# Routing intermediates and bias in PSUM, the blank of the scatter table in parts, rank matmuls one slot later

## The chip, the core and the metric

One core of one Trainium2 chip runs the whole program. Its engines work side by side: PE (TensorE, matmuls and transposes), DVE (VectorE), ACT (ScalarE), POOL (GpSimd) and SP (SyncE, which here only issues DMAs). The metric is the device time of one execution in microseconds; lower is better.

## What is computed

The reference is attention in chunks, then two mixtures of experts (MoE), each of which sends a token to the one expert with the highest logit:

```python
# attention: 8 batches, 8 heads, 576 positions, head size 64, chunks of 64
scores = scale * matmul(q_c, k_c.T)            # 64 x 64 per chunk and head
attn = exp(scores - max); attn /= attn.sum(-1) + 1e-9
x = matmul(attn, v_c)                          # -> x: 4608 tokens x 512
# MoE: 8 experts, 512 -> 1024 -> 512
logits = x @ w_gate + modality_bias[modality_id]
e_idx = argmax(logits)
gate_w = max of softmax(logits)
out[mask] = gate_w * (relu(x[mask] @ w1[e]) @ w2[e])   # for each expert e
# MoE2: the same without bias, for tokens with x @ w_skip > 0, and out = x + y
```

## The kernel before

The change touches the attention stage, about the first 200 us. It walks over 36 tiles of 128 tokens (`for t in range(NTILE)`, L724). One turn of the loop issues, on PE and in this order: the scores of tile t+2 (`sc`, L494, one PSUM bank, one buffer), the transposes of half of the next k (`ps_t<-rk`, L465), the transposes of the probabilities of tile t+1 (`ps_p`, L520), those of the finished rows x of tile t-1 (`ps_x`, L554), those of half of the next q (`ps_t<-rq`), and the product with v (`o_ps`, L529, two PSUM banks, of which each row uses 260 of 512 columns). DVE takes the row maximum `mx` and the difference `e` of the scores, and divides the product by the row sums (`rs`, `x`). ACT takes the exponential and copies out of PSUM. POOL reorders each k and q load (`rk`, `rq`, L457: a sum of two SBUF operands). SP issues all loads.

Every four tiles give a group of 512 tokens, which is routed by the generator `route(gi)` (L566), nine in all. In tiles with t % 4 == 1, from 5 on, PE makes the partial logits (`ps_l`, L560). Then the generator runs in slots: each call of `drip()` in the loop (after `sc`, after `mx`, after `e`, between the three operations of the division, and after them) runs it to its next `yield`, so its instructions lie between those of the tile. In order they are: transposes of the logits (`ps_l2`, named `ps_l` with a number, L571); on DVE their sum `lgt` and the bias added (L578); `gate_argmax`, which is `r_mx`, `r_d` = logits less maximum, `r_er`, on ACT `r_ex` = exp(`r_d`), then `r_mr`, the one-hot choice `r_oh`, the sum `r_sm` of `r_ex`, and its reciprocal into `row`; then `wait2` empty slots; then on PE the rank matmuls `ps_r` (`ranks_mm`, L245, 14 small ones from `r_oh`); on DVE `ranks` (`r_z`, `pos`, `carry`) and `posi`; and on POOL four scatters of `row` into the table `tab` in DRAM (L600).

The pool `ps_l` has one PSUM bank, used in turn by `ps_l`, `ps_l2` and `ps_r`. The intermediates `lgt`, `r_d`, `r_er`, `r_ex`, `r_sm`, `r_z`, `pos` lie in SBUF (pool `rt_p`). Route 3 also picks the fullest expert (`GP` = 3), whose first weight is then loaded, cast by ACT and split (`w1s`, L637) half by DVE and half by POOL in the turns that follow.

Work that is done once, in `g.late`, is run three entries per turn. Among it stands `tables()` (L164), which fills the two tables with a blank by two DMAs on SP, and `bias()` (L175), which computes the bias of all tokens with one transpose and five DVE operations.

Of the kernel before, what the change touches and what calls it, by code (L numbers as in the profile page):

```python
# [131 lines left out]
def setup_late(nc, g, tmp, modality_id, modality_bias, w_gate2, w_skip):  # L132

    NT, NTILE, DM = g.NT, g.NTILE, g.DM
    md = tmp.tile([NTILE, P, 2], I32, name="md")
    nc.gpsimd.dma_start(
        out=md, in_=modality_id.bitcast(I32).rearrange("(t p w) -> t p w", p=P, w=2)
    )
    b01 = tmp.tile([P, 2, E], F32, name="b01")
    nc.gpsimd.dma_start(  # L140
        out=b01.rearrange("p m e -> p (m e)"),
        in_=modality_bias.rearrange("m e -> (m e)").unsqueeze(0).to_broadcast([P, 2 * E]),
    )
# [12 lines left out]
    n = g.NR // P
    m = next(i for i in range(10, 0, -1) if n % i == 0)
    blank0 = tmp.tile([P, n // m, 16], I32, name="blank0")
    nc.gpsimd.memset(blank0, 0)
    nc.gpsimd.memset(blank0[:, :, 0], int(OOB))  # L160
    for t in g.row4:
        nc.gpsimd.memset(t, 0)

    def tables():  # L164
        nc.sync.dma_start(
            out=g.tab[0].rearrange("(p m n) c -> p m (n c)", p=P, m=m),
            in_=blank0.rearrange("p n c -> p (n c)").unsqueeze(1).to_broadcast([P, m, n // m * 16]),
        )
        nc.sync.dma_start(out=g.tab[1].rearrange("(p n) c -> p n c", p=P), in_=blank)

    nop = lambda: None

    mf = tmp.tile([NTILE, P], F32, name="mf")

    def bias():  # L175
        pm = g.ps_l.tile([P, P], F32, tag="l", name="pm")
        nc.tensor.transpose(pm[:, 0:NTILE], mf, g.ident[0:NTILE, 0:NTILE])
        m = tmp.tile([P, NTILE, 2], F32, name="m")
        nc.vector.tensor_copy(m[:, :, 1], pm[:, 0:NTILE])
        nc.vector.tensor_scalar(  # L180
            out=m[:, :, 0], in0=m[:, :, 1], scalar1=-1.0, scalar2=1.0, op0=ALU.mult, op1=ALU.add
        )
        t0 = tmp.tile([P, NTILE, E], F32, name="t0")
        sh = [P, NTILE, E]
        for i, dst in ((0, t0), (1, g.bias)):
            nc.vector.tensor_tensor(
                out=dst,
                in0=m[:, :, i:i + 1].to_broadcast(sh),
                in1=b01[:, i:i + 1, :].to_broadcast(sh),
                op=ALU.mult,  # L190
            )
        nc.vector.tensor_tensor(out=g.bias, in0=g.bias, in1=t0, op=ALU.add)

    def rows():

        pr = g.ps_l.tile([P, DM], F32, tag="l", name="pr")
        for a in range(4):
            nc.tensor.transpose(pr[0:E + 1, a * P:(a + 1) * P], wsm[:, a, :], g.ident)
        rw = tmp.tile([E + 1, DM], F32, name="rw")
        nc.scalar.copy(rw, pr[0:E + 1, :])  # L200
        nc.scalar.dma_start(out=g.rows, in_=rw)

    g.late = [lambda: nc.vector.tensor_copy(mf, md[:, :, 0])] + g.late + [tables, nop, bias, nop, nop, nop, rows]


def gate_argmax(nc, g, pool, lg, n, gate_out, comp=None):

    sh = [P, n, E]  # L210
    mx = pool.tile([P, n], F32, tag="r_mx", name="r_mx")
    nc.vector.tensor_reduce(out=mx, in_=lg, axis=AX.X, op=ALU.max)
    yield
    d = pool.tile(sh, F32, tag="r_d", name="r_d")
    nc.vector.tensor_tensor(out=d, in0=lg, in1=mx.unsqueeze(2).to_broadcast(sh), op=ALU.subtract)  # L215
    yield
    er = pool.tile(sh, F32, tag="r_er", name="r_er")
    nc.vector.scalar_tensor_tensor(
        out=er, in0=d, scalar=0.0, in1=g.rev.unsqueeze(1).to_broadcast(sh),
        op0=ALU.is_ge, op1=ALU.mult,  # L220
    )
    ex = pool.tile(sh, F32, tag="r_ex", name="r_ex")
    nc.scalar.activation(out=ex, in_=d, func=AF.Exp)
    yield
    mr = pool.tile([P, n], F32, tag="r_mr", name="r_mr")
    nc.vector.tensor_reduce(out=mr, in_=er, axis=AX.X, op=ALU.max)
    yield
    oh = pool.tile(sh, BF16, tag="r_oh", name="r_oh")
    if comp is None:
        nc.vector.tensor_tensor(out=oh, in0=er, in1=mr.unsqueeze(2).to_broadcast(sh), op=ALU.is_equal)  # L230
    else:
        nc.vector.tensor_tensor(out=er, in0=er, in1=mr.unsqueeze(2).to_broadcast(sh), op=ALU.is_equal)
        yield
        nc.vector.tensor_tensor(out=oh, in0=er, in1=comp.unsqueeze(2).to_broadcast(sh), op=ALU.mult)
    yield
    sm = pool.tile([P, n], F32, tag="r_sm", name="r_sm")
    nc.vector.tensor_reduce(out=sm, in_=ex, axis=AX.X, op=ALU.add)
    yield
    nc.vector.tensor_scalar(out=sm, in0=sm, scalar1=1e-9, scalar2=None, op0=ALU.add)
    yield  # L240
    nc.vector.reciprocal(out=gate_out, in_=sm.unsqueeze(2))
    return oh
# [9 lines left out]
        nc.tensor.matmul(ps[:, n, :], g.ones, oh[:, s, :], start=(s == 0), stop=(s == n - 1))  # L252


def ranks(nc, g, pool, ps, oh, n, carry, pos):

    sh = [P, n, E]
    z = pool.tile(sh, F32, tag="r_z", name="r_z")
    nc.vector.tensor_tensor(out=z, in0=ps[:, 0:n, :], in1=carry.unsqueeze(1).to_broadcast(sh), op=ALU.add)
    yield  # L260
    nc.vector.tensor_tensor(out=z, in0=z, in1=oh, op=ALU.mult)
    yield
    nc.vector.tensor_reduce(out=pos, in_=z, axis=AX.X, op=ALU.add)
    nc.vector.tensor_tensor(out=carry, in0=carry, in1=ps[:, n, :], op=ALU.add)
    yield
# [119 lines left out]
def attention(ctx, tc, g, q, k, v, w_gate, w1, out, small):  # L385
# [177 lines left out]
            )  # L563
        nc.scalar.copy(g.lsb, ps)

    def route(gi, wait=3, wait2=1):  # L566
        for _ in range(wait):
            yield
        ps = ps_l.tile([P, 4, NA, 32], F32, tag="l", name="ps_l2")
# [5 lines left out]
            out=lgt, in_=ps[:, :, :, 0:E].rearrange("p t a e -> p t e a"), axis=AX.X, op=ALU.add,  # L575
        )
        yield
        nc.vector.tensor_tensor(out=lgt, in0=lgt, in1=g.bias[:, 4 * gi:4 * gi + 4, :], op=ALU.add)  # L578
        row = g.row4[gi % 2]
        nc.gpsimd.tensor_copy(row[:, :, 0], g.tokid[:, 4 * gi:4 * gi + 4])  # L580
        yield
        hot = yield from gate_argmax(nc, g, rt_p, lgt, 4, row[:, :, 1:2].bitcast(F32))
        for _ in range(wait2):
            yield
        ps = ps_l.tile([P, 5, E], F32, tag="l", name="ps_r")
        ranks_mm(nc, g, ps, hot, 4)
# [133 lines left out]
    load_qk(3)  # L720
    reorder(2, "k", nc.vector)
    reorder(2, "q", nc.vector)
    vq = []
    for t in range(NTILE):  # L724
        u = t // 2
# [8 lines left out]
        if t % 2 == 0:  # L734
# [704 lines left out]
```

## Time and profile before

| | |
|---|---|
| median of 3 runs | 967.13 us (966.57 to 968.04) |
| the profiled execution | 967.16 us, of which its span is 965.6 us |
| PE busy | 912.1 us, 94% of the span |
| DVE busy | 647.1 us, 67% |
| ACT busy | 363.0 us, 38% |
| POOL busy | 316.5 us, 33% |

The span runs from the first instruction to the last; what lies around it is 1.6 us. Busy is the time in which the engine works on something, wherever it stands; it does not tell by itself what sets the time. PE's clock is the mean of what the chip granted, 0.985 of full speed over the span.

### The profile page before, as it was taken

The page shows a single profiled execution, that of the slowest core. Times are in us where ns is not written, and L with a number is a line of the kernel's source. Part 1 is how long each engine was busy: PE and PEld are TensorE (multiplying, and loading weights), DVE is VectorE, ACT ScalarE, POOL GpSimd, SP SyncE. Part 2 cuts the span into 40 slices and gives each one's busy share as a digit, 9 for nine tenths or more (in the row PEclk, how much of TensorE's full clock was granted, in tenths as well). Part 3 has the DMA queues.
Part 4 walks back from the last instruction along what each step waited for, and adds up shares of the span by engine and source line. Part 5 has one row for each costly group of instructions (what it writes and reads, how often), then busy time and mean ns, then how long its engine had stood idle before and what let it go on. Part 6 is the DMA issues. An engine that isn't in the chain of part 4 may idle for free. (4 is left out here: it accounts for less than half of the span.)

```text
span 965.6 us, 19576 instructions
## 1 busy us (share of the span) xinstructions
PE 912.1 (94%) x6757; PEld 806.4 (84%) x6757; DVE 647.1 (67%) x1837; ACT 363.0 (38%) x627; POOL 316.5 (33%) x288
## 2 busy tenths in 40 slices
PE   7989998999999999999899999978998999999996
PEld 5767777889999999988699998967897997897995
DVE  7657777687877777996887787777256266625261
ACT  6757787542222222512412222132145155415150
POOL 6464667243233333322322232212211211311210
PEclk9989999999999999999899999989999999999998
DMA  9999996836111111341111134001626456512400
GB/s 216 275 271 229 239 248 164 276 119 237 46 48 55 47 46 56 121 124 49 34 47 46 46 118 150 25 28 27 229 77 244 150 192 234 193 46 93 164 18 16
DMA packets 123098, 121.73 MB, mean 126 GB/s; under 512 B 55565, under 2 KB 94333, under 8 KB 122754
## 3 DMA queue, kind: packets, MB, share of 16 engines
q1 hardware_dynamic: 107344, 84.29, 30.7%
q0 software_dynamic: 14464, 34.43, 10.7%
q8 instruction: 85, 1.39, 0.7%
q14 instruction: 131, 1.07, 0.4%
q10 hardware_dynamic: 1074, 0.54, 0.2%
HBM read 96.37 MB, written 28.72 MB: 130 GB/s over the span
## 5 line engine op out<-in xcount | busy, mean ns | idle before, releaser
L1107 PE MATMUL p<-w2s,hT 128*128 128x512 f32 x1392 | 326.3, 391 | 0.0
L1107 PEld LDWEIGHTS p<-w2s,hT 128*128 128x128 f32 x1392 | 257.8, 188 | 51.9 <-DVEq L1215 0.2
L376 PE MATMUL p<-xTb,w1s 128*128 128x256 f32 x2064 | 264.3, 286 | 12.0 <-DVEq L1328 5.5
L376 PEld LDWEIGHTS p<-xTb,w1s 128*128 128x128 f32 x2064 | 255.8, 194 | 17.0 <-DVE w1s L994 6.1
L1024 DVE CUSTOM_DVE_ANT_0 x<-x,v 128x512 f32<-128x512 f32 x333 | 209.2, 688 | 48.3 <-ACT x L1007 38.4
L1014 POOL DMA_INDIRECT out_dram<-x,ids x56 | 67.6, 1207 | 267.0 <-DVE x L1010 203.0
L1073 ACT ACTIVATE hT<-p 128x512 fp32r<-128x512 f32 x86 | 51.4, 598 | 209.9 <-PE p L376 202.5
L280 POOL DMA_INDIRECT tab<-rowP,posi x38 | 40.6, 1069 | 224.0 <-DVE idsP L1123 177.0
L1074 DVE SCALAR_TENSOR_TENSOR hT<-p,hT 128x512 fp32r<-128x512 f32 x86 | 58.9, 687 | 65.3 <-ACT hT L1073 41.9
L346 POOL DMA_INDIRECT x<-out_dram,ids x68 | 77.0, 1132 | 49.1 <-issue 28.0
L376 PE MATMUL p1t<-xTb,w1s 128*128 128x256 f32 x696 | 87.4, 282 | 0.0
L376 PEld LDWEIGHTS p1t<-xTb,w1s 128*128 128x128 f32 x696 | 84.5, 190 | 0.8 <-issue 0.8
L1007 ACT ACTIVATE x<-p,ids 128x512 f32<-128x512 f32 x33 | 22.7, 688 | 145.8 <-PE p L1107 142.4
L476 ACT COPY kb<-ps_t 64x512 f32<-64x512 f32 x70 | 43.9, 627 | 41.9 <-PE ps_t L465 41.5
L994 DVE TENSOR_TENSOR w2s<-r,w2s 128x512 fp32r<-128x512 f32 x88 | 56.6, 687 | 0.8 <-ACT w2s L992 0.6
L992 ACT CAST w2s<-r 128x512 fp32r<-128x512 f32 x88 | 51.0, 620 | 13.0 <-issue 6.4
L600 POOL DMA_INDIRECT tab<-row,posi x36 | 37.0, 1029 | 51.3 <-DVE x L545 18.7
L1010 DVE SCALAR_TENSOR_TENSOR x<-p,ids,x 128x512 f32<-128x512 f32 x23 | 17.2, 748 | 53.4 <-PE p L1107 48.6
L362 DVE TENSOR_TENSOR xTb<-px,xTb 128x512 fp32r<-128x512 f32 x70 | 44.9, 682 | 11.2 <-ACT xTb L361 10.3
L994 DVE TENSOR_TENSOR w1s<-r,w1s 128x1024 fp32r<-128x1024 f32 x40 | 46.4, 1222 | 2.5 <-ACT w1s L992 2.0
L494 PE MATMUL sc<-kb,Tq 128*64 128x128 f32 x576 | 40.9, 281 | 6.1 <-DVE r_d L215 2.9
L361 ACT CAST xTb<-px 128x512 fp32r<-128x512 f32 x70 | 37.6, 591 | 19.4 <-PE px L359 19.4
(220 smaller groups left out, 1061.3 us busy)
## 6 DMA issues: line engine op xcount, KB each, us to landing
r<-in_moe_w_dram SPq DMA_DIRECT2D x18, 2048.0 KB, 10.0
out_dram<-x SPq DMA_DIRECT2D x9, 1024.0 KB, 6.5
k<-in_k_dram SPq DMA_DIRECT2D x11, 512.0 KB, 5.2
q<-in_q_dram SPq DMA_DIRECT2D x11, 512.0 KB, 7.0
vt<-in_v_dram SPq DMA_DIRECT2D x32, 144.0 KB, 5.5
r<-in_moe_w_dram POOLq DMA_DIRECT2D x2, 2048.0 KB
v<-in_v_dram SPq DMA_DIRECT2D x24, 144.0 KB, 6.0
tab<-blank SPq DMA_DIRECT2D x1, 2320.0 KB, 12.1
```

Of the source, the lines that this page charges most:

```text
L346: return [nc.gpsimd.indirect_dma_start(out=x[:, h, :], out_offset=None, in_=src, in_offset=IOff(ap=ids[:, h, 0:1], axis=0), bounds_check=s ...
L362: nc.vector.tensor_tensor(out=t[:, 1, :, h * P:(h + 1) * P], in0=ps, in1=o.bitcast(F32), op=ALU.subtract)
L376: nc.tensor.matmul(ps, w1s[:, b, kk, f * P:(f + 1) * P], xt[:, a, kk, :], start=(i == 0), stop=(i == 3 * KD - 1),)
L476: eng(kb[u % 2][64 * j:64 * j + 64, sl, j, :].rearrange("p a (c r) -> p a r c", r=2), ps[64 * j:64 * j + 64],)
L494: nc.tensor.matmul(out=ps[64 * c:64 * c + 64, a, :, :], lhsT=T_[u][:, a, cs], rhs=kb[u % 2][:, a, :, cs], start=True, stop=True,)
L992: hi(s[:, 0, kk, :], r[:, kk, :])
L994: eng.tensor_tensor(out=s[:, 1, kk, :], in0=r[:, kk, :], in1=s[:, 0, kk, :].bitcast(F32), op=ALU.subtract)
L1014: b = nc.gpsimd.indirect_dma_start(out=out, out_offset=IOff(ap=ids[:, h, 0:1], axis=0), in_=o[:, h, :], in_offset=None, bounds_check=NT - ...
L1024: nc.vector.tensor_tensor_reduce(out=junk[i % 2], in0=x2[:, h, :], in1=w2g[:, i, :], scale=1.0, scalar=0.0, op0=ALU.mult, op1=ALU.add, acc ...
L1073: nc.scalar.activation(out=o, in_=ps, func=AF.Relu)
L1074: nc.vector.scalar_tensor_tensor(out=l, in0=ps, scalar=0.0, in1=o.bitcast(F32), op0=ALU.max, op1=ALU.subtract)
L1107: nc.tensor.matmul(ps, hT[:, a, f, h * P:(h + 1) * P], w2s[:, b, f, :], start=(f == 0 and i == 0), stop=(f == KF - 1 and i == 2),)
```

## The change

Three things are changed. The one DMA that blanks the first table becomes five parts, issued at the start of turns 2 to 6, and the blank of the second table moves from turn 2 to turn 20. In routes 0 to 7 the biased logits (now `lgb`, L601), `r_d`, `r_er`, `r_sm`, `r_z` and `pos` are columns of the one PSUM bank (`bank`, named `ps_r`) whose first 40 columns take the rank matmuls, so that bank is taken already at the bias; the bias itself is copied once, by eight DVE copies, into free columns of the two `o_ps` banks. `wait2` is 2 where it was 1.

```diff
-    def tables():
+    def table0(i, k):
+        a, b = i * m // k, (i + 1) * m // k
         nc.sync.dma_start(
-            out=g.tab[0].rearrange("(p m n) c -> p m (n c)", p=P, m=m),
-            in_=blank0.rearrange("p n c -> p (n c)").unsqueeze(1).to_broadcast([P, m, n // m * 16]),
-        )
-        nc.sync.dma_start(out=g.tab[1].rearrange("(p n) c -> p n c", p=P), in_=blank)
+            out=g.tab[0].rearrange("(p m n) c -> p m (n c)", p=P, m=m)[:, a:b],
+            in_=blank0.rearrange("p n c -> p (n c)").unsqueeze(1).to_broadcast([P, b - a, n // m * 16]),
+        )
+    g.blanks = {t: (lambda i=i: table0(i, 5)) for i, t in enumerate(range(2, 7))}
+    g.blanks[20] = lambda: nc.sync.dma_start(out=g.tab[1].rearrange("(p n) c -> p n c", p=P), in_=blank)
...
-    g.late = [lambda: nc.vector.tensor_copy(mf, md[:, :, 0])] + g.late + [tables, nop, bias, nop, nop, nop, rows]
+    g.bias_done = bias
+    g.late = [lambda: nc.vector.tensor_copy(mf, md[:, :, 0])] + g.late + [nop, bias, nop, nop, nop, rows]
...
-    d = pool.tile(sh, F32, tag="r_d", name="r_d")
+    d = mk("r_d", [n, E])
-    er = pool.tile(sh, F32, tag="r_er", name="r_er")
+    er = mk("r_er", [n, E])
-    sm = pool.tile([P, n], F32, tag="r_sm", name="r_sm")
+    sm = mk("r_sm", [n])
-    z = pool.tile(sh, F32, tag="r_z", name="r_z")
+    z = mk("r_z", [n, E])
...
-    def route(gi, wait=3, wait2=1):
+    def route(gi, wait=3, wait2=2):
...
-        nc.vector.tensor_tensor(out=lgt, in0=lgt, in1=g.bias[:, 4 * gi:4 * gi + 4, :], op=ALU.add)
+        in_psum = gi < NG - 1
+        bias = bias_ps(gi) if in_psum else g.bias[:, 4 * gi:4 * gi + 4, :]
+        bank = ps_l.tile([P, 512], F32, tag="l", name="ps_r")
+        at = [64]
+        def mk(name, shape):
+            if not in_psum:
+                return rt_p.tile([P] + shape, F32, tag=name, name=name)
+            n = shape[0] * (shape[1] if len(shape) > 1 else 1)
+            t = bank[:, at[0]:at[0] + n]
+            at[0] += n
+            return t.rearrange("p (t e) -> p t e", e=shape[1]) if len(shape) > 1 else t
+        lg0, lgt = lgt, mk("lgb", [4, E])
+        nc.vector.tensor_tensor(out=lgt, in0=lg0, in1=bias, op=ALU.add)
...
-        ps = ps_l.tile([P, 5, E], F32, tag="l", name="ps_r")
+        ps = bank[:, 0:5 * E].rearrange("p (t e) -> p t e", e=E)
-        pos = rt_p.tile([P, 4], F32, tag="pos", name="pos")
+        pos = mk("pos", [4])
...
+    def bias_ps(gi):
+        o = NA * D1 + 4 * E * (gi // 2)
+        return o_ps[:, gi % 2, o:o + 4 * E].rearrange("p (t e) -> p t e", e=E)
+    def bias_copy():
+        for gi in range(NG - 1):
+            nc.vector.tensor_copy(bias_ps(gi), g.bias[:, 4 * gi:4 * gi + 4, :])
...
+        if t in g.blanks:
+            g.blanks[t]()
```

Three places show what this does to the engines' order. A row is line, operation, output and inputs, the output's size, and in brackets the engines whose progress it waits for (their names with a number).

On DVE the gate of route 0, from `r_er` to the reciprocal `row`, between the operations of one tile, before:

```order
L218 SCALAR_TENSOR_TENSOR r_er<-r_d,rev 128x32 [waits DVE_49]
L539 TENSOR_SCALAR rs<-o_ps 128x8 [waits PE_49]
L226 TENSOR_REDUCE r_mr<-r_er 128x4 [waits DVE_49]
L543 RECIPROCAL rs<-rs 128x8 [waits DVE_49]
L230 TENSOR_TENSOR r_oh<-r_er,r_mr 128x32 [waits DVE_49]
L545 TENSOR_TENSOR x_77<-o_ps,rs 128x512 [waits DVE_49]
L237 TENSOR_REDUCE r_sm<-r_ex 128x4 [waits Activation_49]
L239 TENSOR_SCALAR r_sm<-r_sm 128x4 [waits DVE_49]
L241 RECIPROCAL row_87<-r_sm 128x4 [waits DVE_49,Pool_49]
```

And of the change, where `ps_r` is the shared bank:

```order
L225 SCALAR_TENSOR_TENSOR ps_r<-ps_r,rev 128x32 [waits DVE_49]
L547 TENSOR_SCALAR rs<-o_ps 128x8 [waits PE_49]
L233 TENSOR_REDUCE r_mr<-ps_r 128x4 [waits Activation_49]
L551 RECIPROCAL rs<-rs 128x8 [waits DVE_49]
L237 TENSOR_TENSOR r_oh<-ps_r,r_mr 128x32 [waits DVE_49]
L553 TENSOR_TENSOR x_77<-o_ps,rs 128x512 [waits DVE_49]
L244 TENSOR_REDUCE ps_r<-r_ex 128x4 [waits DVE_49]
L246 TENSOR_SCALAR ps_r<-ps_r 128x4 [waits DVE_49]
L248 RECIPROCAL row_87<-ps_r 128x4 [waits DVE_49,Pool_49]
```

The order is the same; the wait for ACT, whose `r_ex` reads `r_d` in the shared bank, has moved from the sum (L237) up to `r_mr` (L233), ahead of the one-hot choice and of the division.

On PE the rank matmuls of route 0, with the last scores ahead of them and the first transposes behind, before (of the 14 weight loads and matmuls, two of each are shown):

```order
L494 MATMUL sc<-kb_173,Tq 64x128 [waits DVE_49,PE_49]
L494 MATMUL sc<-kb_173,Tq 64x128 x7
L248 LDWEIGHTS upper
L248 MATMUL ps_r<-r_oh,upper 128x8 [waits DVE_49]
L248 LDWEIGHTS upper
L248 MATMUL ps_r<-r_oh,upper 128x8
```

And of the change:

```order
L502 MATMUL sc<-kb_173,Tq 64x128 [waits DVE_49,PE_49]
L502 MATMUL sc<-kb_173,Tq 64x128 x7
L255 LDWEIGHTS upper [waits DVE_49]
L255 MATMUL ps_r<-r_oh,upper 128x8 [waits Activation_49]
L255 LDWEIGHTS upper
L255 MATMUL ps_r<-r_oh,upper 128x8
```

They stand at the same place, right behind the scores. In the program before the wait for DVE is met by `r_oh` (L230); in the changed one the count that the first weight load waits for is that of the reciprocal L248, the last operation of the gate that touches the shared bank, and the wait for ACT is that for `r_ex`. The same holds for routes 1, 2, 3, 5 and 6. In route 4 the rank matmuls move from behind `sc` to behind `o_ps` of the same turn, and its `ps_l2` from ahead of `sc` to behind it; in route 7 they move behind the transposes `ps_p`. For route 5 a DVE half of the weight split `w1s` now stands between `lgt` and the added bias.

On SP the loads from the first blank to the loads of v for batch 2 (`v_83`), before:

```order
L165 DMA tab_58<-blank_357 1280x1x464 [waits DMAHW3_49]
L169 DMA tab_59<-blank 128x580 [waits DMAHW4_49]
L437 DMA k<-in_k_dram 96x8x128 [waits DMAHW5_49,Pool_49]
L437 DMA k<-in_k_dram 32x8x128 [waits DMAHW6_49]
L437 DMA q<-in_q_dram 96x8x128 [waits DMAHW7_49,DMAHW2_49,Pool_49]
L437 DMA q<-in_q_dram 32x8x128 [waits DMAHW0_49]
L444 DMA v_83<-in_v_dram 64x9x64 [waits DMAHW1_49,PE_49]
L444 DMA v_83<-in_v_dram 64x9x64 [waits DMAHW2_49]
L660 DMA out_dram<-x_76 128x4x512 [waits DMAHW3_49,DVE_49]
```

And of the change:

```order
L167 DMA tab_58<-blank_357 128x2x464 [waits DMAHW3_49]
L167 DMA tab_58<-blank_357 128x2x464 [waits DMAHW4_49]
L445 DMA k<-in_k_dram 96x8x128 [waits DMAHW5_49,Pool_49]
L445 DMA k<-in_k_dram 32x8x128 [waits DMAHW6_49]
L445 DMA q<-in_q_dram 96x8x128 [waits DMAHW7_49,DMAHW2_49,Pool_49]
L445 DMA q<-in_q_dram 32x8x128 [waits DMAHW0_49]
L167 DMA tab_58<-blank_357 128x2x464 [waits DMAHW1_49]
L452 DMA v_83<-in_v_dram 64x9x64 [waits DMAHW2_49,PE_49]
L452 DMA v_83<-in_v_dram 64x9x64 [waits DMAHW3_49]
L167 DMA tab_58<-blank_357 128x2x464 [waits DMAHW4_49]
L691 DMA out_dram<-x_76 128x4x512 [waits DMAHW5_49,DVE_49]
```

The fifth part comes behind four of the eight loads of v for batch 2 and ahead of the last four, so all five parts are still ahead of those; the blank of the second table is gone from here. The first scatter of route 0 on POOL waits for all five parts.

## Rows read from the trace of the kernel before

**Rows 1.** stretch 200:220: busy us (x count) by engine, clock, DMA share.
```profile
200.00:220.00 20.00, 20.00 (x136) 17.88 (x136) 17.87 (x89) 4.86 (x10) 10.70 (x11) 1.00 0.47 155
```

**Rows 2.** PE timeline: start us, us, line, operation [idle before <-releaser].
```profile
45.63 1.09 PE L494 MATMUL sc<-kb,Tq 128*64 128x128 f32 x16
...
49.49 1.04 PE L494 MATMUL sc<-kb,Tq 128*64 128x128 f32 x16
...
50.47 0.21 PE L248 MATMUL ps_r<-r_oh,upper 128*128 128x8 bf16 x2
...
53.65 0.61 PE L494 MATMUL sc<-kb,Tq 128*64 128x128 f32 x8
```

**Rows 3.** PE timeline, places where it waits, 60 to 160 us.
```profile
64.69 0.44 PE L529 MATMUL o_ps<-v,pt 128*64 128x130 f32 x4 [2.12 <-DMA v<-in_v_dram]
...
66.67 0.70 PE L529 MATMUL o_ps<-v,pt 128*64 128x130 f32 x4 [1.53 <-DMA v<-in_v_dram]
...
68.34 1.98 PE L494 MATMUL sc<-kb,Tq 128*64 128x128 f32 x16
...
74.45 1.04 PE L494 MATMUL sc<-kb,Tq 128*64 128x128 f32 x16
...
93.99 1.09 PE L494 MATMUL sc<-kb,Tq 128*64 128x128 f32 x16 [1.47 <-DVE r_d L215]
...
133.21 0.19 PE L248 MATMUL ps_r<-r_oh,upper 128*128 128x8 bf16 x2 [0.48 <-DVE r_oh L230]
...
137.34 1.09 PE L494 MATMUL sc<-kb,Tq 128*64 128x128 f32 x16 [0.79 <-DVE r_z L259]
...
155.17 0.19 PE L248 MATMUL ps_r<-r_oh,upper 128*128 128x8 bf16 x2 [3.42 <-DVE r_oh L230]
...
159.76 1.04 PE L494 MATMUL sc<-kb,Tq 128*64 128x128 f32 x16
```

**Rows 4.** PE timeline row, then two stretches of 1 us.
```profile
12.65 0.63 PE L465 MATMUL ps_t<-ident,rq 128*128 128x128 f32 x4 [1.99 <-DVE rq L455]
...
12.00:13.00 1.00, 0.35 (x3) 0.39 (x4) 0.97 (x2) 0.00 (x0) 1.00 (x3) 1.00 0.50 117
...
67.00:68.00 1.00, 1.00 (x8) 0.71 (x4) 0.53 (x3) 0.00 (x0) 0.88 (x1) 0.50 0.99 261
```

**Rows 5.** POOL and DVE timelines; then one group of DVE instructions by line.
```profile
90.48 1.90 POOL L457 TENSOR_TENSOR rq<-q,zero 128x1024 f32<-128x1024 f32 x1
...
89.41 3.04 DVE L578 TENSOR_TENSOR lgt<-lgt,bias 128x32 f32<-128x32 f32 x1
...
152.48 1.90 POOL L457 TENSOR_TENSOR rq<-q,zero 128x1024 f32<-128x1024 f32 x1
...
149.88 4.57 DVE L215 TENSOR_TENSOR r_d<-lgt,r_mx 128x32 f32<-128x32 f32 x1
...
L259 DVE TENSOR_TENSOR r_z<-ps_r,carry 128x32 f32<-128x32 f32 x9 | 1.6, 181 | 0.0
```

**Rows 6.** ACT and DVE timelines, end of a gate.
```profile
50.63 0.24 ACT L223 ACTIVATE r_ex<-r_d 128x32 f32<-128x32 f32 x1
...
94.20 0.19 DVE L226 TENSOR_REDUCE r_mr<-r_er 128x4 f32<-128x32 f32 x1
...
95.56 0.18 DVE L241 RECIPROCAL row<-r_sm 128x4 f32<-128x4 f32 x1
```

**Rows 7.** DMA issues, 0:100 us (KB each); DVE timeline of the bias.
```profile
tab<-blank SPq DMA_DIRECT2D x1, 290.0 KB
...
35.98 0.18 DVE L179 COPY m<-pm 128x36 f32<-128x36 f32 x1
...
37.92 0.46 DVE L192 TENSOR_TENSOR bias<-bias,t 128x288 f32<-128x288 f32 x1
```

**Rows 8.** DVE and POOL timelines, start of the weight split.
```profile
134.02 0.69 DVE L637 TENSOR_TENSOR w1s<-stage,w1s 128x512 fp32r<-128x512 f32 x1 [0.75 <-ACT w1s L634]
...
134.07 1.78 POOL L637 TENSOR_TENSOR w1s<-stage,w1s 128x512 fp32r<-128x512 f32 x1 [5.04 <-ACT w1s L634]
```

More of the change, by code (lines that the diff above doesn't have):

```diff
@@ L201, in rows, with gate_argmax @@
         nc.scalar.dma_start(out=g.rows, in_=rw)
-    g.late = [lambda: nc.vector.tensor_copy(mf, md[:, :, 0])] + g.late + [tables, nop, bias, nop, nop, nop, rows]
-def gate_argmax(nc, g, pool, lg, n, gate_out, comp=None):
+    g.bias_done = bias
+    g.late = [lambda: nc.vector.tensor_copy(mf, md[:, :, 0])] + g.late + [nop, bias, nop, nop, nop, rows]
+def gate_argmax(nc, g, pool, lg, n, gate_out, comp=None, mk=None):
     sh = [P, n, E]
+    mk = mk or (lambda name, shape: pool.tile([P] + shape, F32, tag=name, name=name))
     mx = pool.tile([P, n], F32, tag="r_mx", name="r_mx")
@@ L252, in ranks_mm, with ranks @@
         nc.tensor.matmul(ps[:, n, :], g.ones, oh[:, s, :], start=(s == 0), stop=(s == n - 1))
-def ranks(nc, g, pool, ps, oh, n, carry, pos):
+def ranks(nc, g, pool, ps, oh, n, carry, pos, mk=None):
     sh = [P, n, E]
-    z = pool.tile(sh, F32, tag="r_z", name="r_z")
+    mk = mk or (lambda name, shape: pool.tile([P] + shape, F32, tag=name, name=name))
+    z = mk("r_z", [n, E])
     nc.vector.tensor_tensor(out=z, in0=ps[:, 0:n, :], in1=carry.unsqueeze(1).to_broadcast(sh), op=ALU.add)
@@ L581, in route @@
         yield
-        hot = yield from gate_argmax(nc, g, rt_p, lgt, 4, row[:, :, 1:2].bitcast(F32))
+        hot = yield from gate_argmax(nc, g, rt_p, lgt, 4, row[:, :, 1:2].bitcast(F32), mk=mk)
         for _ in range(wait2):
             yield
-        ps = ps_l.tile([P, 5, E], F32, tag="l", name="ps_r")
+        ps = bank[:, 0:5 * E].rearrange("p (t e) -> p t e", e=E)
         ranks_mm(nc, g, ps, hot, 4)
         yield
-        pos = rt_p.tile([P, 4], F32, tag="pos", name="pos")
-        yield from ranks(nc, g, rt_p, ps, hot, 4, g.carry[0], pos)
+        pos = mk("pos", [4])
+        yield from ranks(nc, g, rt_p, ps, hot, 4, g.carry[0], pos, mk)
         posi = rt_p.tile([P, 4], I32, tag="posi", name="posi")
@@ L722, in attention @@
     reorder(2, "q", nc.vector)
+    g.late.insert(g.late.index(g.bias_done) + 1, bias_copy)
     vq = []
```

## The prediction

> **What bounds the kernel now.** I first took busy time by stretches. Behind attention PE is full: from 200 to 220 us it works 20.00 of 20 us [rows 1]. What attention gains or loses there is therefore passed on to the end, and the question is only what PE does in the first 200 us. There I read PE's timeline, and take as measure the distance from one tile's `sc` to the next.
>
> An undisturbed tile takes 45.63 to 49.49, which is 3.86 us. The tile of route 0 with its rank matmuls takes 49.49 to 53.65, 4.16 us: the ranks start at 50.47 with no idle time ahead of them, and from them to the next `sc` it is 3.18 us [rows 2]. So ranks cost 0.3 us when nothing is late, and the attention stage is PE-bound too, apart from the waits that the next view shows [rows 3]:
>
> - At 64.69 and 66.67 PE waits 2.12 and 1.53 us for v, 3.65 together. Then the clock falls: from 67 to 68 it is 0.50 [rows 4], the level of 1.2 GHz. The tile from 68.34 to 74.45 takes 6.11 us, 2.25 above the plain one, and the 1.67 us from 66.67 to 68.34 ran at half speed, so half of them, 0.83, is lost. With the waits this place costs 6.73 us.
> - At 93.99 PE waits 1.47 us for `r_d` of route 2. The same wait comes once more for route 3. The cause is beside it: the bias addition takes 3.04 us from 89.41 and ends just after POOL's `rq`, which runs from 90.48 to 92.38 [rows 5].
> - Route 4 costs 0.48 + 0.79 = 1.27 us, for `r_oh` and `r_z`.
> - Route 5: at 155.17 the ranks wait 3.42 us for `r_oh`, because `r_d` at 149.88 took 4.57 us, until POOL's `rq` of 152.48 was done [rows 5]. From the ranks to the next `sc` at 159.76 it is 4.59 us instead of 3.18: another 1.41 at the lower clock. Together 4.83.
>
> Routes 0, 1 and 6 lose nothing at their ranks.
>
> **What the change removes.** A DVE operation with one operand in PSUM was not held: `r_z<-ps_r,carry` took 181 ns on the mean of nine [rows 5]. The bias addition and `r_d` become such operations, and the 3 and 4.6 us above should fall to about 0.18. By itself this gives back up to 2 x 1.47 + 1.27 + 4.83 = 9.0 us.
>
> The 290 KB blank of the second table leaves the queue ahead of the v loads [rows 7]. In the stretch of that wait the queue moved 261 GB/s [rows 4], so it is worth 297/261 = 1.1 us of v's arrival. The other table's five parts have the same bytes and all still stand ahead of the last four v loads; I cost their splitting at nothing.
>
> **What it adds: a wait of PE at every route.** The ranks now wait for the whole gate, down to the reciprocal into `row`, and the gate's `r_mr` waits for `r_ex` on ACT. Before, the ranks waited for `r_oh` alone. In route 0, `r_ex` starts at 50.63 and ends at 50.87; from `r_mr` to the end of the reciprocal it is 94.20 to 95.74, 1.54 us, in an undisturbed gate [rows 6], the division of one tile (`rs`, `x`) among it. With two hand-overs of 0.04 and 0.05 us (an estimate) the ranks can start at 52.50. PE is there at 50.47 [rows 2]. So PE stalls 2.03 us in each route whose ranks stand right behind `sc`: 0, 1, 2, 3, 5 and 6. All that is behind PE's ranks waits as well: `ps_t<-rk`, `ps_p`, `ps_x`, `o_ps`. The extra slot of `wait2` doesn't help, since the ranks stand at the same place in PE's order.
>
> The Trainium skill (PSUM — Partial Sum Buffer, "PSUM bank collisions raise a hardware error") says that PSUM is to be guarded by bank, or by bank and quarter of the partitions, and not by address, two readers included. That is the rule that speaks against this change: columns 64 and up are not free for DVE and ACT while PE writes columns 0 to 39. No run here shows it yet; by it these six stalls stay, and without it they would not be there.
>
> **The sum, place by place** (after less before):
>
> - *Up to the v wait.* PE comes 2.03 us later out of route 0. The bias moves one turn up: `m<-pm` at 35.98 to the end of `bias<-bias` at 38.38 is 2.40 us of DVE [rows 7], now in a turn that already has other late work, and the eight copies, at 0.18 each by the nearest row [rows 5], add 1.4 in the next. PE waits for neither directly but for `e` behind them. Bounds are 0 and 2.40; I take 0.9, since most of it was ahead of `e` in the old place too. So PE arrives 2.9 us later, and v 1.1 earlier, against a wait of 3.65: the wait is gone, and with it, I take it, the fall of the clock. From -6.73 of losses to +2.9: **-3.8**. Bounds: -4.2 with no bias cost (0.5 of the wait is then left), -2.3 with all of it; and -0.7 if the clock still falls.
> - *Route 1.* **+2.0**.
> - *Routes 2 and 3.* 2.03 in place of 1.47, twice: **+1.1**.
> - *Route 4.* Its ranks come behind `o_ps`, so most of the gate is over by then. But the weight split `w1s` (0.69) [rows 8], `mx` and `e` of the next tile stand ahead of its reciprocal on DVE. I take a wait of 0.7 in place of 1.27: **-0.5**. Bounds -0.65 and +5 (the second rival).
> - *Route 5.* DVE's `w1s` now stands between the sum `lgt` and the bias addition. It has two operands in SBUF and will wait for POOL's `rq`, whose end is 154.38 [rows 5], as `r_d` did; then follows the gate. The hold goes from one instruction to another: **0**. Bounds: -2.2, if the split slips in ahead of POOL, which leaves 2.03 and a little for the split where 4.83 stood; +1.3, if the whole gate is late behind it.
> - *Route 6.* **+2.0**.
> - *Route 7.* Ranks behind `ps_p`, half a tile later: a small rest of the stall, **+0.3**.
>
> The sum is +1.1 on 967.16, the profiled run's own time, which lies 0.03 above the median of the three runs: **968.3 us**. A change of less than 0.2% (1.9 us, so 965.2 to 969.1) cannot be told from none with this kernel. The forecast lies in that band: what POOL no longer holds up is paid back in waits for the bank.
>
> **The rivals.**
>
> *A. The ranks wait no longer than before.* If the stall of 2.03 us is not there (the last operations of the gate run as early as `r_oh`, or ACT's `r_ex` no longer stands behind `e`), the stalls of routes 1, 2, 3 and 6 go. At v PE is then only 0.9 later, 1.65 of the wait is left, and with the clock kept up that place gives -1.1 - 3.08 = -4.2. Routes 2 and 3 give -2.9, route 4 -0.5: together -7.6, and -10 with route 5 at its lower end: **957 to 960**. For it: the port waits are real, and ACT has spare time. Against it: `r_ex` itself started 0.16 us after the ranks in route 0, at 50.63, and the wait for it is in the program. 15%.
>
> *B. DVE loses its place to POOL at route 4's split.* Before, DVE's half started at 134.02 and POOL's at 134.07, 50 ns apart [rows 8]. If POOL is first, DVE waits, and POOL's next two pieces are `rk` and `rq`, with no scatter between them in this turn: POOL's `w1s` took 1.78, of which 0.64 was DVE's hold, and the others take 1.9 each [rows 5]. So DVE waits 1.14 + 3.80 = 4.9 us, with `mx`, `e` and the reciprocal queued behind, and PE behind those. The price is 4.9, and with a fall of the clock as in route 5 (1.41) 6.3: **973 to 975**. It decides from those 50 ns on. 15%.
>
> *C. The clock falls at each stall.* A PE wait of 1.99 us at 12.65 left the clock at 1.00, a wait of 3.42 us and one of 2.12 and 1.53 in a row were followed by 0.50 [rows 3, 4]. The new stalls are 2.03, next to the first. If each of five costs 1.4 as in route 5: +7, **975**. 8%.
>
> *D. Splitting the blank doesn't help v.* The v loads come no earlier, or part of the wait and the low clock stay: +2 to +3 on the forecast, **970 to 971**. The rate in the queue is what it was, so the loads' order could cost as much as the 290 KB give. 12%.
>
> **How the numbers follow.** The forecast's own case, 50%, reaches from 966 to 970 by the bounds of the bias, of routes 4 and 5; about 36 of these 50 fall within 965.2 to 969.1, 10 above and 4 below. Faster: 15 (A) + 4 + 3 for routes 4 and 5 both at their lower ends = 22%. Slower: B 15, C 8, D 12 less 5 that stay inside the band, and 10: 40%; I give 37. The rest, 41%, is no change. The range takes in D and B whole and the nearer side of A, and leaves out most of A and C: **962 to 974**.
>
> **What would show it.** Right, if PE's timeline has a wait of about 2 us ahead of `ps_r` in routes 0, 1, 2, 3 and 6, put down to `row` (L248) or what stands just before it on DVE; the additions at L601 and L222 take about 0.2 us each, beside `rk` and `rq` too; the wait for v near 65 us is under 1 us and no tile there takes 6 us; and DVE's split ahead of route 5's bias addition takes over 3 us. Wrong, if ranks follow `sc` without a gap (A), if `w1s` near 134 us takes over 4 us (B), if the clock shows 0.50 behind the 2 us waits (C), or if PE still waits for v by 2 us or more (D). The prediction fails most easily at route 4, where 50 ns decide over 5 us, and at the place of the v wait, where two arrivals within 0.5 us of each other decide over 3 us of clock.

## The result and the profile after

The changed kernel is slower: 980.09 us (979.22 to 982.80) against 967.59 us (966.57 to 970.88), a ratio of 1.0121 with a 95% interval of 1.0090 to 1.0152. The forecast was 968.3, with a range of 962 to 974. The profiled execution took 979.80 us, with a span of 978.2. The kernel before took between 967.6 and 975.2 us from one series of runs to the next, so below every kernel is compared with the kernel before of its own series, by ratio.

The timeline of PE, changed kernel, answers to [rows 2] and [rows 3]. The columns are start, length, line, operation, and in brackets the idle time ahead of it and what ended it; x16 means that 16 such instructions are merged in the row.

```profile
31.20 1.09 PE L502 MATMUL sc<-kb,Tq 128*64 128x128 f32 x16
...
39.30 1.97 PE L502 MATMUL sc<-kb,Tq 128*64 128x128 f32 x16 [4.07 <-DVE rs L547]
...
46.28 1.09 PE L502 MATMUL sc<-kb,Tq 128*64 128x128 f32 x16
...
51.98 1.09 PE L502 MATMUL sc<-kb,Tq 128*64 128x128 f32 x16
...
58.90 0.20 PE L255 MATMUL ps_r<-r_oh,upper 128*128 128x8 bf16 x2 [2.01 <-DVE row L248]
...
78.86 0.20 PE L255 MATMUL ps_r<-r_oh,upper 128*128 128x8 bf16 x2 [2.01 <-DVE row L248]
...
98.77 0.21 PE L255 MATMUL ps_r<-r_oh,upper 128*128 128x8 bf16 x2 [1.96 <-DVE row L248]
...
103.61 1.04 PE L502 MATMUL sc<-kb,Tq 128*64 128x128 f32 x16
...
141.11 0.20 PE L255 MATMUL ps_r<-r_oh,upper 128*128 128x8 bf16 x2 [0.58 <-DVE rs L547]
...
160.76 0.22 PE L255 MATMUL ps_r<-r_oh,upper 128*128 128x8 bf16 x2 [4.75 <-DVE row L248]
...
165.35 1.04 PE L502 MATMUL sc<-kb,Tq 128*64 128x128 f32 x16
...
181.65 0.21 PE L255 MATMUL ps_r<-r_oh,upper 128*128 128x8 bf16 x2 [1.94 <-DVE row L248]
```

The new wait that was forecast, of 2.0 us, is there at routes 0, 1, 2 and 6, put down to `row`; route 3 has one more of 1.96 (at 119.94, not shown). The waits for v and for `r_d` are gone; `r_d` took 0.19 us at 154.13, beside POOL's weight split. Two things were not forecast in this size: 4.07 us ahead of the scores at 39.30, and 4.75 at route 5.

The gate of route 0 in the changed kernel, on ACT and on DVE, which answers to [rows 6]:

```profile
56.98 0.21 ACT L230 ACTIVATE r_ex<-ps_r 128x32 f32<-128x32 f32 x1
```

```profile
57.22 0.19 DVE L233 TENSOR_REDUCE r_mr<-ps_r 128x4 f32<-128x32 f32 x1 [1.00 <-ACT r_ex L230]
...
57.45 0.19 DVE L237 TENSOR_TENSOR r_oh<-ps_r,r_mr 128x32 bf16<-128x32 f32 x1
...
58.66 0.18 DVE L248 RECIPROCAL row<-ps_r 128x4 f32<-128x4 f32 x1
```

`r_mr` waits for `r_ex` to end, `r_oh` is there 0.4 us later, and the ranks still don't start before `row` ends at 58.84.

What stands behind the 4.07 us is on DVE and POOL, changed kernel:

```profile
32.86 0.18 DVE L184 TENSOR_SCALAR m<-m 128x36 f32<-128x36 f32 x1
33.08 2.12 DVE L190 TENSOR_TENSOR t<-m,b 128x288 f32<-128x288 f32 x1
35.12 2.14 DVE L190 TENSOR_TENSOR bias<-m,b 128x288 f32<-128x288 f32 x1
37.30 0.46 DVE L196 TENSOR_TENSOR bias<-bias,t 128x288 f32<-128x288 f32 x1
37.68 0.68 DVE L511 TENSOR_REDUCE mx<-sc 128x8 f32<-128x512 f32 x1
```

```profile
32.99 1.90 POOL L465 TENSOR_TENSOR rk<-k,zero 128x1024 f32<-128x1024 f32 x1 [3.65 <-PE ps_t L473]
34.84 2.11 POOL L465 TENSOR_TENSOR rq<-q,zero 128x1024 f32<-128x1024 f32 x1
```

The two multiplications of the bias, each with two operands in SBUF, lie beside POOL's `rk` and `rq` and take 2.1 us each. In the kernel before, where they stood a turn later, they took less than 0.5:

```profile
37.06 0.46 DVE L186 TENSOR_TENSOR t<-m,b 128x288 f32<-128x288 f32 x1
37.43 0.45 DVE L186 TENSOR_TENSOR bias<-m,b 128x288 f32<-128x288 f32 x1
```

`mx` and `e` are queued behind them, and PE's next scores wait for `e` to empty their bank.

Route 5 in the changed kernel, DVE:

```profile
157.61 3.00 DVE L660 TENSOR_TENSOR w1s<-stage,w1s 128x512 fp32r<-128x512 f32 x1
160.53 0.17 DVE L248 RECIPROCAL row<-ps_r 128x4 f32<-128x4 f32 x1
```

The DVE half of a weight split, which took 0.69 us at 152.10, takes 3.00 here. It lies beside POOL's `rq` (156.81 to 158.72) and POOL's own half of the split (158.79 to 160.05), and ends 0.56 us after that half. `row` stands behind it, and the ranks wait for `row`.

Two stretches of the changed kernel, busy time by engine, then clock, DMA share and GB/s:

```profile
39.00:40.00 1.00, 0.70 (x8) 0.73 (x10) 0.93 (x4) 0.63 (x1) 1.00 (x1) 0.50 1.08 383
...
100.00:101.00 1.00, 1.00 (x7) 1.00 (x6) 0.12 (x2) 0.72 (x2) 0.00 (x0) 0.50 1.40 184
```

The clock is at 1.2 GHz (0.50) behind the 4.07 us, behind one of the five waits of 2 us, that of route 2, and behind the 4.75 of route 5 (0.50 from 161 to 163).

### The profile page after: what moved, and what is told of

Same layout as the page of the kernel before. It is cut to its first block, busy times and chain, and to the rows that moved or that the text cites. A ratio compares the mean times of both kernels' runs of the same rounds, so it can differ in the third digit from the quotient of the medians.

```text
span 978.2 us, 19576 instructions
## 1 busy us (share of the span) xinstructions
PE 919.1 (94%) x6757; PEld 813.3 (83%) x6757; DVE 635.3 (65%) x1845; ACT 363.0 (37%) x627; POOL 311.8 (32%) x288
## 5 line engine op out<-in xcount | busy, mean ns | idle before, releaser
L1048 POOL DMA_INDIRECT out_dram<-x,ids x56 | 63.4, 1132 | 269.9 <-DVE x L1044 206.5
```

Source lines behind the costliest of these rows:

```text
L1048: b = nc.gpsimd.indirect_dma_start(out=out, out_offset=IOff(ap=ids[:, h, 0:1], axis=0), in_=o[:, h, :], in_offset=None, bounds_check=NT - ...
```

## The experiments

**Ranks and their bank.** f3 takes the last three operations of the gate (the sum, the addition of 1e-9 and the reciprocal) out of the ranks' bank:

```diff
-    sm = mk("r_sm", [n])
+    sm = pool.tile([P, n], F32, tag="r_sm", name="r_sm")
```

> The changed kernel with one edit: the sum r_sm of the gate lies in SBUF again, so that the gate's last three operations no longer touch the bank of the ranks. Theory, that the ranks wait for the last operation that touches their bank: that is now r_oh, which comes about 0.45 us after the end of r_ex, and the wait of 2.0 us falls to 0.8 to 0.9 in routes 0, 1, 2, 3 and 6; 5 x 1.15 = 5.8 us less than the changed kernel, ratio 1.005 to 1.008. Rival, that the ranks wait because DVE's gate is late as a whole: the wait stays at 2 us, now put down to r_oh, ratio 1.012.

f2 is the changed kernel in the same series, f1 the kernel before.

> The changed kernel once more, unchanged, beside the others of this call. Theory, that the loss comes from the waits of 2.0 us at the ranks and the wait of 4 us behind the bias, both set by the program's order: the same waits at the same places, ratio 1.010 to 1.015. Rival, that a good part of the loss came from the clock after those waits, which may fall at other places: the waits are the same but the ratio moves to 1.005 or 1.018, with the difference in the stretches of lower clock.

> The kernel before once more, unchanged, to have its trace beside those of the others of this call. Every theory: the time of the kernel before of this call, within 0.5%. What it shows is whether PE's waits in attention (3.65 us for v, 1.47 twice, 1.27 and 3.42 us at the routes) stand at the same places when the whole time is some us longer.

Measured: f3 0.9987 (0.9964 to 1.0010), f2 1.0091 (1.0061 to 1.0121), f1 1.0007 (0.9981 to 1.0032). PE in f3 at route 0:

```profile
57.55 0.21 PE L255 MATMUL ps_r<-r_oh,upper 128*128 128x8 bf16 x2 [0.81 <-DVE r_oh L237]
```

The wait is 0.81 to 0.83 us in routes 0, 1, 2, 3, 5 and 6, as the bank theory gave it, and now put down to `r_oh`. One tile of [128, 4] floats in another memory is worth 1% of the program. The ratio came out below the range expected, 1.005 to 1.008: besides the 5.8 us of shorter waits, route 2's low clock (7.77 us for its tile in f2, 5.05 here) and 1.5 us at route 5 go as well, and f2's attention is 8.8 us longer than f3's. The wait behind the bias is still there in f3, with 3.99 us.

The Trainium skill (PSUM — Partial Sum Buffer, "PSUM bank collisions raise a hardware error") has the rule to guard PSUM by bank, or by bank and quarter of the partitions, and not by address. The program's waits follow it by bank: in f3 1.2 us of the 2.0 went with the three operations that left the bank.

h1 makes the PSUM part alone, with blanks, bias turn and `wait2` as before; h2 keeps the change but blanks as before; h3 and h4 are the two kernels in that series.

> The kernel before with the PSUM part of the change alone: tables blanked as before, the bias in its old turn (the eight copies behind it), wait2 = 1. Theory, that the loss is the shared bank: waits of 2.0 us at the ranks of routes 0, 1, 2, 3 and 6 put down to the last operation of the gate, a wait for v shortened by them, ratio 1.006 to 1.012. Rival, that the other parts (blank, wait2) make the loss, 0.5% each when tried alone: the ratio is 1.000 to 1.004.

> The changed kernel with the tables blanked as before, the bias staying one turn early. Theory, that the blank in parts is worth nothing here, because PE comes to v late anyway by the waits ahead of it: the wait for v is below 1 us, ratio within 0.002 of the changed kernel's in this call. Rival, that the blank in parts costs by itself (POOL's first scatter waits for the last part, and its reorders land on the gate of route 1): 0.003 to 0.006 less than the changed kernel.

> The changed kernel as the measure of this call. Every theory: ratio 1.009 to 1.015, waits of 2.0 us at the ranks of routes 0, 1, 2, 3 and 6.

> The kernel before as the measure of this call, for its trace. Every theory: the time of the kernel before of this call, within 0.5%, with the waits for v and at routes 2, 3, 4 and 5 as far as POOL's reorders fall on the same gate operations.

Measured: h1 1.0175 (1.0137 to 1.0214), h2 1.0199 (1.0161 to 1.0237), h3 1.0163 (1.0121 to 1.0204), h4 1.0006 (0.9985 to 1.0027). The PSUM part, without the other two, loses as much as the whole change in this series. It is not the ranks' bank alone, since the bias copies in the `o_ps` banks belong to it: PE's product waits 1.98 us for them. Its ratio lies above the range expected, as does that of the changed kernel itself in this series, and its waits at the ranks run from 1.2 to 4.6 us in routes 0 to 6, where 2.0 was expected. The blank in parts neither adds nor saves anything that can be told.

In h3 the waits at the ranks are 2.01 in route 0, 2.6 to 3.0 in routes 1 to 3, 3.85 in route 5 and 1.62 in route 6. In route 1 PE stands from 75.93, and ACT comes to `r_ex` at 77.06, 1.13 us later; in route 0 of the first trace it was 0.09 later (56.98, and 58.90 less 2.01). So the price of the bank is not a constant; here it grew with the time at which ACT came to `r_ex`.

**Moving the ranks instead.** In e3 each route waits until the product with v of its turn is issued (the lines that set `g.av` are left out here):

```diff
+        while gi < NG - 1 and not g.av:
+            yield
         ps = bank[:, 0:5 * E].rearrange("p (t e) -> p t e", e=E)
```

> The changed kernel with the rank matmuls of routes 0 to 7 behind the product with v of the same turn, about 3.2 us of PE work later. Theory: the ranks wait for the whole gate because it lies in their bank, and the gate is over 2.0 us after the scores; behind that work no wait of 2 us is left in routes 0, 1, 2, 3 and 6, which gives back 10 us less what the wait for v takes back near 70 us (up to 2) and the place of route 2's low clock: time 969 to 973. Rival, that the gate is late on DVE and any place waits for it, or that the later positions hold up the scores of the next tile: waits of 1 to 2 us stay in those tiles, time 977 to 981.

Measured: 1.0113 (1.0075 to 1.0151). The waits of 2 us are gone, 0.48 us at `ps_x` is left of them. But the ratio lies among those of the changed kernel (1.009 to 1.016 in three series; this series has no run of it): in route 5 PE's product with v waits 4.11 us for the bias addition L601, which reads the bias out of `o_ps`'s bank and stands behind a `w1s` of 4.18 us, and at three tiles the transposes of the logits wait 1.1 to 1.7 us for ACT's copy `lsb`. The rival's time, 1.010 to 1.014 as a ratio, came true by another mechanism.

**The bias turn.** e1 puts bias and copies back one turn:

```diff
-    g.late = [lambda: nc.vector.tensor_copy(mf, md[:, :, 0])] + g.late + [nop, bias, nop, nop, nop, rows]
+    g.late = [lambda: nc.vector.tensor_copy(mf, md[:, :, 0])] + g.late + [nop, nop, bias, nop, nop, rows]
```

e2 leaves them where the change has them and puts one operand (m) in PSUM:

```diff
-        pm = g.ps_l.tile([P, P], F32, tag="l", name="pm")
+        pm = g.ps_l.tile([P, 512], F32, tag="l", name="pm")
...
-        m = tmp.tile([P, NTILE, 2], F32, name="m")
+        m = pm[:, P:P + 2 * NTILE].rearrange("p (n c) -> p n c", c=2)
```

> The changed kernel with the bias and its copies one turn later, the turn in which the bias stood before. Theory: the two bias multiplications of 2.1 us each were held by POOL's reorder of k and q beside them; one turn later they take about 0.46 each, the wait of 4.07 us ahead of the scores near 39 us falls under 1 us, and no low clock follows it. PE then comes to the loads of v about 5 us earlier and waits there again, by my estimate 1 to 3 us. Time 975 to 978. Rival, that the wait comes from the number of operations in that turn and the copies: the wait moves one turn on and stays over 2 us, time 979 to 981.

> The changed kernel with one operand of the two bias multiplications (m) in PSUM, at the same place. Theory of the held port: the multiplications take about 0.46 us each in place of 2.1, beside the same POOL work, and the wait ahead of the scores near 39 us falls from 4.07 to about 0.8 (4.07 less 3.3). Time 975 to 978. Rival, that the number of operations makes the wait: they keep about 2 us each, the wait stays at 4, time 980.

Measured: e1 1.0132 (1.0097 to 1.0167), e2 1.0148 (1.0123 to 1.0173). DVE and POOL in e2:

```profile
32.83 0.46 DVE L190 TENSOR_TENSOR t<-pm,b 128x288 f32<-128x288 f32 x1
33.20 0.45 DVE L190 TENSOR_TENSOR bias<-pm,b 128x288 f32<-128x288 f32 x1
33.68 1.42 DVE L196 TENSOR_TENSOR bias<-bias,t 128x288 f32<-128x288 f32 x1
```

```profile
32.90 1.89 POOL L465 TENSOR_TENSOR rk<-k,zero 128x1024 f32<-128x1024 f32 x1 [3.85 <-DVE pm L184]
34.75 2.11 POOL L465 TENSOR_TENSOR rq<-q,zero 128x1024 f32<-128x1024 f32 x1
```

With an operand in PSUM the multiplications take 0.46 us beside the same POOL work, and the hold passes to the third operation, which still has both in SBUF; PE's wait falls from 4.07 to 1.70. So what made the multiplications long was the second operand in SBUF. The Trainium skill (SBUF — State Buffer, "Who interferes with whom") states that a DVE instruction with two SBUF inputs contends with a GpSimd instruction that reads SBUF; the 2.12 and 0.46 us agree with it.

In e1 the multiplications take 0.46 and 0.45 us and the wait ahead of the scores is gone, but a second cost shows: the eight copies write to `o_ps`, and PE's product waited 2.14 us for them. Neither ratio lies clearly below those of the changed kernel, and this series has no run of it to compare with. PE comes earlier to the next places and finds other waits there: in both, `ps_x` waits 1.1 us at the tiles ahead of routes 2 and 3, the scores of a tile ahead of route 4 wait 1.3 us for ACT's copy `Tq`, and the ranks of route 5 wait 3.9 us. What makes each of them was not tried.

**The small parts alone.** g2 is the kernel before with one edit:

```diff
-    def route(gi, wait=3, wait2=1):
+    def route(gi, wait=3, wait2=2):
```

e4 and g3 are the kernel before with the blanks alone moved, as in the change's diff.

> The kernel before with only the blank of the table in five parts and the second table's blank moved to turn 20. My forecast's term: v comes 1.1 us earlier, the wait of 3.65 us for v shrinks to about 2.5, and the clock may stay up: time 963 to 966.5. Rival, that the parts ahead of the last v loads cost as much as they give: wait of 3.5 or more, time 967 to 968.

> The kernel of e4 once more (only the blanks moved), beside the others of this call: e4 gave 1.003, which says little. Theory, that the parts help v by the 290 KB: the two waits for v sum to 1 us less than in the kernel before, ratio 0.997 to 1.000. Rival, that they only shift what is late: ratio 1.001 to 1.004, with a new wait at a later route.

> The kernel before with wait2 = 2 as its only edit. Theory, that this slot alone moves nothing that PE waits for except at routes 4 and 7: ratio 0.999 to 1.002, the waits at routes 2, 3 and 5 as before. Rival, that it is worth something by itself: the wait of 3.4 us at route 5 or that of 1.3 at route 4 goes, ratio 0.995 to 0.998.

Measured: e4 1.0029 (1.0008 to 1.0050), g3 1.0055 (1.0023 to 1.0087), g2 1.0060 (1.0038 to 1.0082). All three are slower than their theories said. The wait for v was 2.31 us in e4 and 1.01 in g3. The kernel before has 3.65 in [rows 3], but 2.28 in f1 and 2.36 in h4, so e4 shows no gain, and g3 one of about 1.3 against those two (0.5 against g2, which has 1.53 in the same series with the blank as before). What was lost is at route 1, where PE waits 2.90 us in e4 and 4.96 in g3. POOL and DVE in g3:

```profile
62.58 1.09 POOL L604 DMA_INDIRECT tab<-row,posi  x1 [12.10 <-DMA v<-in_v_dram]
...
71.24 1.91 POOL L461 TENSOR_TENSOR rk<-k,zero 128x1024 f32<-128x1024 f32 x1
73.09 1.91 POOL L461 TENSOR_TENSOR rq<-q,zero 128x1024 f32<-128x1024 f32 x1
```

```profile
70.79 4.27 DVE L234 TENSOR_TENSOR r_oh<-r_er,r_mr 128x32 bf16<-128x32 f32 x1
```

The first scatter, which waits for all five parts, comes at 62.58 after 12.1 us of idle time (put down to a transfer of v that landed with them); in f1 it came at 55.78. The same holds inside one series: g1, with the blank in parts, has its first scatter at 65.47, and g4, which differs from it by the blank alone, at 56.80. POOL's queue slips, and in g3 its next `rk` and `rq` fall on `r_oh`, for which PE waits 4.96 us. In f1 they came 3.2 us earlier and fell on `r_d` (2.50 us at 69.39) while PE ran at a clock of 0.50 behind the wait for v, and PE had no wait at route 1. For g2 no such chain is shown: its waits for `r_d` at routes 2 and 3 are 2.0 and 2.6 us where h4, in another series, has 1.3; whether the slot makes that or the moment of POOL's reorders was not told apart.

**Versions without the waits.** f4 is f3 with `r_ex` issued behind `ps_x` and so ahead of e's exponential (`r_er` moves one slot up with it), and m in PSUM. g1 also leaves out the addition of 1e-9 in routes 0 to 7 and puts `t` in PSUM. g4 is g1 with the blanks as before. The part of the edit that issues `r_ex`, which the gate has put into the list `g.exq`, behind `emit_xT(t - 1)`:

```diff
+        while g.exq:
+            g.exq.pop(0)()
```

> The changed kernel with three edits: r_sm in SBUF again, ACT's r_ex issued ahead of the exponential e of its turn instead of behind it, and one operand of the two bias multiplications in PSUM. Theory: r_oh is then where it stood in the kernel before, the ranks of routes 0, 1, 2, 3 and 6 follow the scores with less than 0.3 us of wait, the wait of 4 us behind the bias falls to 1.7 or less, and what the waits for POOL's port cost is gone: 10 to 13 us less than the changed kernel, ratio 0.995 to 1.001. Rival, that other waits take their place (for v, for ACT's copies, for the bias in the o_ps banks): ratio 1.004 or more with waits of 1 us and over at those places.

> The kernel of f4 with two more edits: in routes 0 to 7 the addition of 1e-9 to r_sm is left out (the sum holds exp(0) = 1, so in float32 it changes nothing), and the third operation of the bias has an operand in PSUM too. Theory: that addition, SBUF to SBUF with one input, was held 3.80 us by POOL's rk and rq in route 1, and behind it the next scores waited 2.71 us; this wait goes. The wait behind the bias falls from 2.97 to 2.0 to 2.5. About 3 us less than f4, less what v's loads take back: ratio to the kernel before 0.992 to 0.996. Rival, that the next operation on DVE is held in its place: a wait of 2 to 3 us stays at route 1, ratio 0.996 to 0.999.

> The kernel of g1 with the tables blanked as in the kernel before (one DMA of 2320 KB and one of 290 KB in turn 2). Theory, that the blank in parts matters once PE no longer comes late to v: the waits for v near 65 us sum to 1 to 3 us more than in g1 and the clock falls after them, ratio 0.002 to 0.005 above g1. Rival, that v's arrival is set by the same bytes either way: no difference over 0.001 and waits for v within 0.5 us of g1's.

Measured: f4 0.9968 (0.9941 to 0.9995), g1 0.9972 (0.9949 to 0.9996), g4 0.9963 (0.9939 to 0.9988). These three beat both kernels, by about 3 us the one before. In f4 the ranks of routes 0 to 3 have no wait at all. The wait behind the bias is 2.97 us, where 1.7 or less was expected: two small copies into `carry` in that turn took 1.97 us together, 0.23 in the changed kernel. One wait is new, at route 1; DVE and POOL there:

```profile
74.26 3.80 DVE L257 TENSOR_SCALAR r_sm<-r_sm 128x4 f32<-128x4 f32 x1
```

```profile
74.26 1.93 POOL L477 TENSOR_TENSOR rk<-k,zero 128x1024 f32<-128x1024 f32 x1
76.11 1.92 POOL L477 TENSOR_TENSOR rq<-q,zero 128x1024 f32<-128x1024 f32 x1
```

An addition to four numbers per partition lasts as long as both of POOL's reorders, 3.80 us where it took 0.17 at this route in f3, and the scores behind it wait 2.71. g1 leaves it out, which the expectation put at 3 us; nothing of that is seen in the ratio. There route 1 waits 2.10 us for `r_oh`, and in route 5 the hold is on the next instruction:

```profile
149.24 6.16 DVE L673 TENSOR_TENSOR w1s<-stage,w1s 128x512 fp32r<-128x512 f32 x1
155.32 0.18 DVE L614 TENSOR_TENSOR ps_r<-lgt,o_ps 128x32 f32<-128x32 f32 x1
```

PE's product waits 5.22 us for L614, because the bias lies in its bank: the rival's case, and its ratio, with the wait at another route. g4 against g1 shows no difference for the blank (0.9963 and 0.9972, intervals overlapping), though v's waits are 1.81 and 1.27 us; its expectation's rival fits.

## Why the prediction was wrong

The direction of the main term was right, and its size too: 2.03 us was forecast for each route whose ranks stand behind `sc`, 1.94 to 2.01 measured in five of six. The two hand-overs in it, put at 0.04 and 0.05 us, measured 0.03 (57.19 to 57.22) and 0.06 (58.84 to 58.90) in route 0. Place by place (distances between `sc` rows, after less before, in the first pair of traces and in the second, f2 less f1), forecast and measured:

| place | forecast | measured | second pair |
|---|---|---|---|
| up to route 1's scores | -3.8 | 75.81 - 74.45 = +1.4 | +4.5 |
| route 1 | +2.0 | +2.1 | +1.9 |
| routes 2 and 3 | +1.1 | +1.9 | +1.9 |
| route 4 | -0.5 | -1.2 | -1.1 |
| route 5 | 0 | +1.4 | 0.0 |
| route 6 and 7 | +2.3 | +2.0 | +2.0 |
| attention | +1.1 | +7.6 | +9.2 |

**The step that failed** is the bias in the first of these terms, "Bounds are 0 and 2.40; I take 0.9". The three tiles from 31.20 to 51.98 took 20.78 us where they had taken 14.74, from the first of these rows of the kernel before to its scores at 45.63 [rows 2]:

```profile
30.89 1.04 PE L494 MATMUL sc<-kb,Tq 128*64 128x128 f32 x16
...
39.93 1.09 PE L494 MATMUL sc<-kb,Tq 128*64 128x128 f32 x16 [0.28 <-DVE rs L539]
```

That is +6.0 in place of 0.9. The wait ahead of the scores makes 3.8 of it (4.07 in place of 0.28), and the tile at the lower clock behind it most of the rest. The term comes out alike in the other pairs: +5.8 from f1 to f2, +4.9 from h4 to h3. I gave the moved operations the durations of their old place, 2.40 in all, as the upper bound. The rule that I applied to the gate, that an operation with two SBUF operands is held beside `rk` and `rq`, was not applied to them, though their new place lies beside POOL's reorders of the same turn. The bound should have been about 2.4 + 3.3 and a fall of the clock. That v's wait vanished, with its low clock, was right, and it hid 6.7 of the lost microseconds in the first pair; in f1 that loss was smaller (2.28 us of wait), so the second pair shows +4.5 at this place.

What the term is worth to the whole program is another question, and the runs do not bear out that it is 6 us. e2 brought the same tiles to 15.93 us, and its ratio, in another series, was 1.0148; f3 left them at 20.91 and was as fast as the kernel before (0.9987), once the ranks no longer waited for `row`. So the bank's waits, which were forecast in their size, are what the loss hangs on; the forecast went wrong in what it set against them.

**Route 5** failed in its place: the split at the bias addition was not held (0.69 us), the next one was, ahead of `row`. The bound of +1.3 was just passed. **Rival C** came in at one of five waits (route 2, +1.6). **Rival B** did not: DVE kept its place, 138.85 against 138.90 on POOL. **Rival A** is nearest to f4, where the ranks' stalls are gone as in A. Its 957 to 960 was too good: it counted 1.65 us of wait for v, and f4 has 1.32 there, but f4 also waits 2.97 us behind the bias with the clock at 0.50 after it, 2.71 at route 1 and 2.37 for v at 154.64, none of them in A.

**Behind attention** the first pair differs by another 5.0 us (12.6 of span less 7.6). In f1 and f2 it is 0.4 (9.6 of span less 9.2), in h3 and h4 2.6 (17.4 less 14.8). In the first pair, waits of the same length (2.35 and 2.39 us for x, 2.16 and 2.46 ahead of the last experts) are followed by a low clock in the trace after alone (0.50 and 0.61, against 1.00). So these 5 us are not shown to belong to the change, and the ratio of 1.012 holds some of them.

What the ratio of a kernel was worth moved with the series: the changed kernel gave 1.0121, 1.0091 and 1.0163. What differs between series in the traces is when DMAs land and so where POOL's reorders fall. That this is the cause was not tested. The series also ran at different times and not all on the same chip, and nothing here tells these apart.

## What to carry to other kernels

Scratch in free columns of a PSUM bank that PE writes made PE wait here for the last operation on the bank, and not for its own operand (2.0 us in place of 0.8 in f3): put there only what PE's input depends on anyway, and count the operations behind it in the bank's order. When an operation moves, give it the durations of its new neighbours: one with two SBUF operands lasted as long as POOL's work beside it (2.12 us beside 1.90), and in e2 the next such operation inherited the hold (1.42). Removing one of many short waits in a chain that is bound by several late arrivals brought up other waits here (e1, e2, e3, g1), so judge it by the end of the stage.

## What the runs showed of the hardware

A `TENSOR_SCALAR` of 128x4, with one SBUF input, took 3.80 us beside POOL's `rk` and `rq` in f4, and 2.53 beside `rq` and a weight split at route 5 of f3; at route 1 of f3, outside POOL's reorders, it took 0.17. A multiplication of 128x288 with an operand in PSUM ran in 0.46 us beside POOL work that made it 2.12 with both in SBUF. How long a hold lasts differs: that multiplication ended at 35.20 in the changed kernel, 0.31 us after `rk` and while `rq` ran, but the addition in f4 ended only with both over (78.06, and 78.03 for `rq`). The Trainium skill (SBUF — State Buffer, "Who interferes with whom") lists `tensor_scalar` among the operations that can take the ports shared with GpSimd; the 3.80 and 2.53 us agree with it.

Waits of nearly one length, 1.94 to 2.02 us, were followed by the clock of 1.2 GHz in one case of five, the same one (route 2) in the first trace and in f2; the tile behind it took 7.84 and 7.77 us in place of 6.2.
